# Image chunks in pairs in a fused attention and feed-forward kernel: one bank of turned sums, one key product, one copy

## The chip, the cores and the metric

The kernel runs on one core of a Trainium2 chip. The metric is the device time of one execution in microseconds (us), quoted as the median of several runs. The span that the profile shows is about 1.8 us shorter than the timed figure of the same run.

## The reference

```python
kv_pool = kv.reshape(B, H // 4, 4, W // 4, 4, C).mean(axis=(2, 4))   # B=4, H=384, W=32, C=128
k = v = kv_pool.reshape(B, -1, C) @ w_sr                             # 768 keys per image
a = softmax(q @ k.T / sqrt(C))                                       # q: 12288 tokens per image
x = a @ v
out = (relu(x @ w_gate) * (x @ w_val)) @ w_out                       # 128 -> 1536 -> 128
```

Each image of 384 by 32 pixels is averaged over 4 by 4 squares to 768 keys, in six chunks of 128. Each key serves as its own value. 49152 tokens attend to the keys of their image and go through a gated feed-forward layer.

## The kernel before

Tokens go in 96 tiles of 512. For a tile, TensorE makes six score blocks (one per image chunk), ScalarE takes the exponential, TensorE weights the values, and later turns them through the feed-forward layer (12 value products, 12 gate products, 48 output products). A chunk must be pooled before any score: its pixels lie as 16 blocks of 128x128 (four image lines times four columns) to be added, turned so that channels lie on partitions, multiplied by `w_sr`, scaled into keys, and turned back into values.

```python
def add_lines(eng, b, jc, i):                  # sums of image lines, one chunk
    ...
    eng.tensor_tensor(s2[:, i], parts[:, 2 * i], parts[:, 2 * i + 1], op=ALU.add)
    ...
def turn_pooled(b, jc, pooled):                # TensorE turns and adds what is left, one bank a chunk
    tp = bank([128, 128])
    n = pooled.shape[1]
    for i in range(n):
        nc.tensor.matmul(tp, pooled[:, i, :], ident, is_transpose=True,
                         start=(i == 0), stop=(i == n - 1))
    keep_turned(b, jc, tp)                     # copy on VectorE
def project(b, jc):                            # key product, then keep_keys: scaled copy on VectorE
    key_banks[b, jc] = bank([128, 128])
    nc.tensor.matmul(key_banks[b, jc], w_sr_f32, kv_Ts.pop((b, jc)), start=True, stop=True)
...
def keep_values(k, half, copy=nc.vector.tensor_copy):
    ...
    nc.vector.reciprocal(rinvs[k][:, own], x_ps[:, :, C])
    if half == 1:
        ...
        nc.vector.tensor_tensor(inv2s[k][:, :, 0], rinv, rinv, op=ALU.mult)   # the squaring
```

In the start, where nothing else is ready, TensorE turns and adds all 16 blocks of chunks 0 and 1 of image 0, the lines of chunks 2 to 5 are summed on VectorE first (one sum on GpSimd), and the scores of four tiles are made chunk by chunk. In the steady part the next image is pooled on GpSimd while tiles 16 to 21 of an image's 24 take the pooled chunks in.

The softmax here doesn't subtract the row's maximum and nothing guards it: scores larger than these inputs give would overflow.

## Time and profile before

| | before |
|---|---|
| time, median of 3 (lowest, highest) | 1053.98 us (1052.41, 1054.56) |
| span of the profiled run | 1051.8 us |
| first exponential; first value product of the feed-forward layer | 14.42; 34.84 us |
| a tile without, with image work | 10.51; 10.90 us |
| squarings on VectorE, 128x4 | 96, least 161, median 163, most 1218 ns |

The first value product marks the end of the start: from there TensorE goes tile by tile. A tile's length is read from its first value product to that of the next. The columns of a line in part 5 of the page are the line, engine and operation, the shapes, the count, then busy us and mean ns of one, then the idle time ahead of it.

### The profile page before, as it was taken

The page shows a single profiled execution, that of the slowest core. Times are in us where ns is not written, and L with a number is a line of the kernel's source. Part 1 is how long each engine was busy: PE and PEld are TensorE (multiplying, and loading weights), DVE is VectorE, ACT ScalarE, POOL GpSimd, SP SyncE. Part 2 cuts the span into 40 slices and gives each one's busy share as a digit, 9 for nine tenths or more (in the row PEclk, how much of TensorE's full clock was granted, in tenths as well). Part 3 has the DMA queues.
Part 4 walks back from the last instruction along what each step waited for, and adds up shares of the span by engine and source line. Part 5 has one row for each costly group of instructions (what it writes and reads, how often), then busy time and mean ns, then how long its engine had stood idle before and what let it go on. Part 6 is the DMA issues. An engine that isn't in the chain of part 4 may idle for free.

```text
span 1051.8 us, 26213 instructions
## 1 busy us (share of the span) xinstructions
PE 1035.5 (98%) x9988; PEld 690.8 (66%) x9988; DVE 922.1 (88%) x1803; ACT 911.8 (87%) x1758; POOL 107.2 (10%) x127
## 2 busy tenths in 40 slices
PE   7999999999999999999999999999999999999997
PEld 4666666666666666666666666666666666666664
DVE  3798989898989898998989898999898989898996
ACT  3988888888888888888888888888888888888886
POOL 2000045200000015400000003340000000000000
PEclk9999999999999999999999999999999999999999
DMA  8843356231322335523224134542341423222111
GB/s 293 126 81 67 74 187 161 57 86 32 86 53 66 71 126 143 154 52 72 66 52 86 32 86 130 169 125 50 72 84 33 87 51 67 51 46 51 46 32 46
DMA packets 125710, 90.76 MB, mean 86 GB/s; under 512 B 103312, under 2 KB 103952, under 8 KB 125584
## 3 DMA queue, kind: packets, MB, share of 16 engines
q1 hardware_dynamic: 120144, 75.85, 27.4%
q0 software_dynamic: 5440, 13.24, 7.7%
q8 instruction: 78, 1.28, 0.5%
q14 instruction: 48, 0.39, 0.1%
HBM read 52.76 MB, written 25.17 MB: 74 GB/s over the span
## 4 chain that ended last, share of the span: by engine, by line
PE 96%; DMA 2%; DVE 1%; ACT 1%; issue 0%; SPq 0%; ACTq 0%; DVEq 0%
PE bank_ps L270 24%; PE bank_ps L256 24%; PE bank_ps L245 24%; PE bank_ps L212 12%; PE bank_ps L200 12%; DMA parts<-in_kv_dram 2%; PE bank_ps L155 0%; PE bank_ps L180 0%; ACT aT L201 0%; DVE hT L259 0%; DVE kv_s L141 0%; ACT o_sb L280 0%; DVE kv_s L138 0%; PE bank_ps L189 0%; DVE x L221 0%
## 5 line engine op out<-in xcount | busy, mean ns | idle before, releaser
L259 DVE SCALAR_TENSOR_TENSOR hT<-bank_ps,val 128x512 f16<-128x512 f32 x1152 | 765.4, 687 | 98.9 <-ACT val L249 70.4
L249 ACT CAST val<-bank_ps 128x512 f16<-128x512 f32 x1152 | 678.0, 590 | 118.0 <-PE bank_ps L245 115.7
L270 PEld LDWEIGHTS <-hT 128*128 128x128 f16 x4608 | 351.0, 98 | 206.3 <-DVE hT L259 2.9
L270 PE MATMUL bank_ps<-wo,hT 128*128 128x128 f16 x4608 | 443.6, 219 | 2.1 <-DVE hT L259 2.0
L245 PE MATMUL bank_ps<-xT,wv 128*128 128x512 f16 x1152 | 436.9, 379 | 0.4 <-ACT x L221 0.4
L256 PE MATMUL bank_ps<-xT,wg 128*128 128x512 f16 x1152 | 435.9, 378 | 0.9 <-DVE hT L259 0.8
L201 ACT ACTIVATE aT<-bank_ps 128x512 f16<-128x512 f32 x576 | 346.2, 604 | 5.8 <-PE bank_ps L200 5.3
L212 PE MATMUL bank_ps<-kv,aT 128*128 128x129 f16 x2304 | 223.7, 220 | 0.0
L212 PEld LDWEIGHTS <-aT 128*128 128x128 f16 x2304 | 177.5, 98 | 68.1 <-issue 0.4
L200 PE MATMUL bank_ps<-qT,kv 128*128 128x512 f16 x576 | 217.6, 381 | 2.7 <-DVE qT L110 1.5
L256 PEld LDWEIGHTS <-wg 128*128 128x128 f16 x1152 | 111.5, 97 | 65.4
L245 PEld LDWEIGHTS <-wv 128*128 128x128 f16 x1152 | 112.7, 98 | 0.6 <-issue 0.5
L221 DVE CAST x<-bank_ps 128x256 f16<-128x256 f32 x186 | 77.2, 415 | 2.1 <-PE bank_ps L212 2.1
L77 POOL DMA_DIRECT2D q<-in_q_dram x23 | 12.5, 543 | 551.0 <-DMA qT<-q 550.8
L138 POOL TENSOR_TENSOR kv_s<-parts 128x512 f32<-128x512 f32 x37 | 46.6, 1271 | 166.3 <-DMA parts<-in_kv_dram 163.9
L282 DVE TENSOR_TENSOR o_sb<-bank_ps,inv 128x512 f32<-128x512 f32 x93 | 63.3, 681 | 0.0
L200 PEld LDWEIGHTS <-kv 128*128 128x128 f16 x576 | 56.4, 98 | 5.5 <-DVE qT L110 2.2
L222 DVE RECIPROCAL rinv<-bank_ps 128x2 f32<-128x2 f32 x192 | 30.8, 160 | 1.0 <-ACT x L221 0.7
L141 POOL TENSOR_TENSOR kv_s<-kv_s 128x512 f32<-128x512 f32 x18 | 22.8, 1268 | 1.4
L226 DVE TENSOR_TENSOR inv<-rinv 128x4 f32<-128x4 f32 x96 | 18.5, 192 | 3.3
L176 DVE COPY kvT<-bank_ps 128x128 f32<-128x128 f32 x24 | 6.8, 284 | 9.4 <-PE bank_ps L166 5.1
L146 POOL TENSOR_TENSOR s<-kv_s 128x256 f32<-128x256 f32 x18 | 13.1, 726 | 1.4
(41 smaller groups left out, 102.0 us busy)
## 6 DMA issues: line engine op xcount, KB each, us to landing
parts<-in_kv_dram SPq DMA_DIRECT2D x48, 512.0 KB, 6.4
out_dram<-o_sb SPq DMA_DIRECT2D x96, 256.0 KB, 2.2
q<-in_q_dram POOLq DMA_DIRECT2D x23, 512.0 KB, 5.2
xT<-x SPq DMA_TRANSPOSE x94, 2.4
q<-in_q_dram SPq DMA_DIRECT2D x1, 768.0 KB, 8.5
wv<-in_moe_w_val_dram POOLq DMA_DIRECT2D x2, 192.0 KB, 4.3
wg<-in_moe_w_gate_dram POOLq DMA_DIRECT2D x2, 192.0 KB, 5.0
wo<-in_moe_w_out_dram POOLq DMA_DIRECT2D x1, 384.0 KB, 9.7
```

The source lines that it names most:

```text
L138: eng.tensor_tensor(s2[:, i], parts[:, 2 * i], parts[:, 2 * i + 1], op=ALU.add)
L200: nc.tensor.matmul(s_ps, kv16[:, k // NST, jc, 0:C], qT_of(k), start=True, stop=True)
L201: nc.scalar.activation(aTs[k][:, jc, :], s_ps, AF.Exp, scale=qk_scale)
L212: nc.tensor.matmul(x_ps[:, i, :], aTs[k][:, jc, s * 128 : (s + 1) * 128], kv16[:, k // NST, jc, C : 2 * C + 1], start=(jc == 0 and i == 0) ...
L221: copy(x16s[k][:, own, :], x_ps[:, :, 0:C])
L222: nc.vector.reciprocal(rinvs[k][:, own], x_ps[:, :, C])
L245: nc.tensor.matmul(va_ps, wv16[:, fb * 128 : (fb + 1) * 128], xTs[k], start=True, stop=True)
L249: nc.scalar.copy(val, va_ps)
L256: nc.tensor.matmul(g_ps, wg16[:, fb * 128 : (fb + 1) * 128], xTs[k], start=True, stop=True)
L259: nc.vector.scalar_tensor_tensor(hTs[k][:, fb, :], g_ps, 0.0, vals.pop((k, fb)), op0=ALU.max, op1=ALU.mult)
L270: nc.tensor.matmul(o_ps[:, s, :], hTs[k][:, fb, s * 128 : (s + 1) * 128], wo16[:, fb, :], start=(fb == 0 and s == 0), stop=(fb == NFB - 1) ...
L282: nc.vector.tensor_tensor(o_sb, o_ps, inv2.to_broadcast([128, NS, 128]), op=ALU.mult)
```

## The change

Its intent: fewer handovers in the start. Two chunks share a bank of turned sums, a key product of 256 columns and each copy. In pair 0 TensorE turns and adds all lines; in pairs 1 and 2 other engines add lines 0 and 1 and TensorE turns lines 2 and 3 as they land. The casts of the first queries and, in the start, the copies of values go from ScalarE to VectorE. The scores of the last pair are made tile by tile, so that tile 0 is finished while the others' exponentials run. In the steady part the same functions run per pair, in 9 tiles instead of 18.

```diff
-        nc.scalar.copy(q16, q32s[i])
+        nc.vector.tensor_copy(q16, q32s[i])
...
+    def turn_open(b, pair):
+        kv_Ts[b, pair] = bank([128, 2, 128])
+    def turn_add(b, pair, lines, first=False, final=False):
...        # for both chunks h and all columns i
+                nc.tensor.matmul(kv_Ts[b, pair][:, h], lines[:, h, i], ident, is_transpose=True, ...)
+        if final:
+            nc.vector.tensor_copy(kvT, kv_Ts[b, pair])
+    def project(b, pair):
+        pr = bank([128, 2, 128])
+        nc.tensor.matmul(pr, w_sr_f32, kv_Ts.pop((b, pair)), start=True, stop=True)
+        nc.vector.tensor_scalar(kv16[:, b, 2 * pair : 2 * pair + 2, 0:C], pr, 1.0 / (r * r), None, ...)
...        # the start, pair 1 (pair 2 alike, with GpSimd and VectorE)
+    s2 = add_lines(1, (nc.vector, nc.vector))
+    turn_open(0, 1)
+    turn_add(0, 1, s2, first=True)
+    attend(0, 0)
+    turn_add(0, 1, line(1, 2))
+    turn_add(0, 1, line(1, 3), final=True)
+    attend(1, 0)
+    project(0, 1)
...        # the last pair, tile by tile
+    for jc in range(4, NJC):
+        scores(0, jc)
+    turn_values(0, 2)
+    for jc in range(4, NJC):
+        scores(1, jc)
+    attend(0, 2)
...
```

More of the change, by code (lines that the diff above doesn't have):

```diff
@@ L127, in kv_load @@
             nc.sync.dma_start(parts[:, dh].rearrange("p h dw c -> p (h dw c)"), rows[dh])
-        for h in range(2):
-            kv_in[b, 2 * pair + h] = parts[:, :, h]
-    s2s, s1s, kv_Ts, key_banks = {}, {}, {}, {}
-    def add_lines(eng, b, jc, i):
-        if i == 0:
-            s2s[b, jc] = work.tile([128, 2, r, C], FP32, tag="kv_s2", bufs=2, name="kv_s2")
-        parts, s2 = kv_in[b, jc], s2s[b, jc]
-        if i < 2:
-            eng.tensor_tensor(s2[:, i], parts[:, 2 * i], parts[:, 2 * i + 1], op=ALU.add)
-        else:
-            s1s[b, jc] = work.tile([128, r, C], FP32, tag="kv_s1", bufs=2, name="kv_s1")
-            eng.tensor_tensor(s1s[b, jc], s2[:, 0], s2[:, 1], op=ALU.add)
-            del kv_in[b, jc], s2s[b, jc]
@@ L144, in pool_columns @@
-    def pool_columns(eng, s1):
-        s2 = work.tile([128, 2, C], FP32, tag="kv_c2")
-        eng.tensor_tensor(s2, s1[:, 0:2], s1[:, 2:4], op=ALU.add)
-        s3 = work.tile([128, 1, C], FP32, tag="kv_c1", bufs=3)
-        eng.tensor_tensor(s3, s2[:, 0:1], s2[:, 1:2], op=ALU.add)
-        return s3
-    def turn_pooled(b, jc, pooled):
-        tp = bank([128, 128])
-        n = pooled.shape[1]
-        for i in range(n):
-            nc.tensor.matmul(
-                tp, pooled[:, i, :], ident, is_transpose=True,
-                start=(i == 0), stop=(i == n - 1),
-            )
-        keep_turned(b, jc, tp)
@@ L161, in turn_lines @@
-    def turn_lines(b, pair):
-        tps = [bank([128, 128]) for _ in range(2)]
-        for dh in range(r):
-            for h in range(2):
-                for dw in range(r):
-                    nc.tensor.matmul(
-                        tps[h], kv_in[b, 2 * pair + h][:, dh, dw, :], ident, is_transpose=True,
-                        start=(dh == dw == 0), stop=(dh == dw == r - 1),
-                    )
-        for h in range(2):
-            del kv_in[b, 2 * pair + h]
-            keep_turned(b, 2 * pair + h, tps[h])
@@ L174, in keep_turned @@
-    def keep_turned(b, jc, tp):
-        kv_Ts[b, jc] = work.tile([128, 128], FP32, tag="kvT", bufs=3, name="kvT")
-        nc.vector.tensor_copy(kv_Ts[b, jc], tp)
-    def project(b, jc):
-        key_banks[b, jc] = bank([128, 128])
-        nc.tensor.matmul(key_banks[b, jc], w_sr_f32, kv_Ts.pop((b, jc)), start=True, stop=True)
-    def keep_keys(b, jc):
-        nc.vector.tensor_scalar(
-            kv16[:, b, jc, 0:C], key_banks.pop((b, jc)), 1.0 / (r * r), None, op0=ALU.mult
-        )
-    def turn_values(b, jc, copy):
-        vt = bank([128, 128], FP16)
-        nc.tensor.transpose(vt, kv16[:, b, jc, 0:C], ident16)
-        copy(kv16[:, b, jc, C : 2 * C], vt)
@@ L193, with pool_pixels @@
-    aTs, x_banks, x16s, xTs, rinvs, inv2s = {}, {}, {}, {}, {}, {}
+        kv_in[b, pair] = parts
+    s3s, kv_Ts, key_banks = {}, {}, {}
+    def pool_pixels(eng, b, pair, h):
+        parts = kv_in[b, pair]
+        s2 = work.tile([128, 2, r, C], FP32, tag="kv_s2", bufs=2)
+        for i in range(2):
+            eng.tensor_tensor(s2[:, i], parts[:, 2 * i, h], parts[:, 2 * i + 1, h], op=ALU.add)
+        s1 = work.tile([128, r, C], FP32, tag="kv_s1", bufs=2)
+        eng.tensor_tensor(s1, s2[:, 0], s2[:, 1], op=ALU.add)
+        c2 = work.tile([128, 2, C], FP32, tag="kv_c2", bufs=2)
+        eng.tensor_tensor(c2, s1[:, 0:2], s1[:, 2:4], op=ALU.add)
+        if h == 0:
+            s3s[b, pair] = work.tile([128, 2, C], FP32, tag="kv_s3", bufs=2, name="kv_s3")
+        eng.tensor_tensor(s3s[b, pair][:, h], c2[:, 0], c2[:, 1], op=ALU.add)
@@ new lines, in turn_open @@
+    def turn_open(b, pair):
+        kv_Ts[b, pair] = bank([128, 2, 128])
+    def turn_add(b, pair, lines, first=False, final=False):
+        n = lines.shape[2]
+        for h in range(2):
+            for i in range(n):
+                nc.tensor.matmul(
+                    kv_Ts[b, pair][:, h], lines[:, h, i], ident, is_transpose=True,
+                    start=(first and h == i == 0), stop=(final and i == n - 1),
+                    skip_group_check=True,
+                )
+        if final:
+            kvT = work.tile([128, 2, 128], FP32, tag="kvT", bufs=2)
+            nc.vector.tensor_copy(kvT, kv_Ts[b, pair])
+            kv_Ts[b, pair] = kvT
@@ new lines, in project, with turn_values @@
+    def project(b, pair):
+        pr = bank([128, 2, 128])
+        nc.tensor.matmul(pr, w_sr_f32, kv_Ts.pop((b, pair)), start=True, stop=True)
+        nc.vector.tensor_scalar(
+            kv16[:, b, 2 * pair : 2 * pair + 2, 0:C], pr, 1.0 / (r * r), None, op0=ALU.mult
+        )
+    def turn_values(b, pair):
+        vt = bank([128, 2, 128], FP16)
+        for h in range(2):
+            nc.tensor.transpose(vt[:, h], kv16[:, b, 2 * pair + h, 0:C], ident16)
+        nc.vector.tensor_copy(kv16[:, b, 2 * pair : 2 * pair + 2, C : 2 * C], vt)
@@ L194 @@
+    aTs, x_banks, x16s, xTs, rinvs, inv2s, sums = {}, {}, {}, {}, {}, {}, {}
     hTs, o_banks, vals = {}, {}, {}
@@ L216, in values, with keep_values @@
             )
-    def keep_values(k, half, copy=nc.vector.tensor_copy):
+    def keep_values(k, half, copy=nc.vector.tensor_copy, now=True):
         own = slice(2 * half, 2 * half + 2)
@@ L221, in keep_values, with keep_sums @@
         copy(x16s[k][:, own, :], x_ps[:, :, 0:C])
-        nc.vector.reciprocal(rinvs[k][:, own], x_ps[:, :, C])
-        if half == 1:
-            rinv = rinvs.pop(k)
-            inv2s[k] = work.tile([128, NS, 1], FP32, tag="inv2", bufs=8, name="inv2")
-            nc.vector.tensor_tensor(inv2s[k][:, :, 0], rinv, rinv, op=ALU.mult)
+        sums[k, half] = x_ps[:, :, C]
+        if now:
+            keep_sums(k, half)
+    def keep_sums(k, half):
+        nc.vector.reciprocal(rinvs[k][:, 2 * half : 2 * half + 2], sums.pop((k, half)))
+        if half == 0:
+            return
+        rinv = rinvs.pop(k)
+        inv2s[k] = work.tile([128, NS, 1], FP32, tag="inv2", bufs=8, name="inv2")
+        nc.vector.tensor_tensor(inv2s[k][:, :, 0], rinv, rinv, op=ALU.mult)
     def x_turn(k):
@@ L318, with attend, line, add_lines @@
         nc.tensor.matmul(idle, ident16, ident16, start=True, stop=True)
-    def attend(jc, tiles=(0, 1)):
-        for k in tiles:
+    def attend(k, pair):
+        for jc in (2 * pair, 2 * pair + 1):
             for half in range(2):
                 values(k, jc, half)
+    def line(pair, dh):
+        return kv_in[0, pair][:, dh]
+    def add_lines(pair, engines):
+        s2 = work.tile([128, 2, r, C], FP32, tag="kv_s2", bufs=2)
+        for h in range(2):
+            engines[h].tensor_tensor(
+                s2[:, h], line(pair, 0)[:, h], line(pair, 1)[:, h], op=ALU.add
+            )
+        return s2
     q_cast(0)
     q_turn_pe(0)
+    turn_open(0, 0)
+    for dh in range(r):
+        turn_add(0, 0, line(0, dh), first=dh == 0, final=dh == r - 1)
+    project(0, 0)
     for i in range(1, GRP):
         q_cast(i)
-    turn_lines(0, 0)
-    for jc in range(2):
-        project(0, jc)
-        keep_keys(0, jc)
-    add_lines(nc.vector, 0, 2, 0)
     for jc in range(2):
         scores(0, jc)
-        turn_values(0, jc, nc.scalar.copy)
+    turn_values(0, 0)
     for i in range(1, GRP):
         q_turn_pe(i)
-    for jc in range(2):
-        for k in range(1, GRP):
+    for k in range(1, GRP):
+        for jc in range(2):
             scores(k, jc)
-    attend(0)
-    add_lines(nc.vector, 0, 3, 0)
-    add_lines(nc.vector, 0, 2, 1)
-    add_lines(nc.vector, 0, 2, 2)
-    turn_pooled(0, 2, s1s.pop((0, 2)))
-    attend(1, [0])
-    add_lines(nc.vector, 0, 3, 1)
-    project(0, 2)
-    add_lines(nc.vector, 0, 3, 2)
-    keep_keys(0, 2)
-    add_lines(nc.gpsimd, 0, 4, 0)
+    s2 = add_lines(1, (nc.vector, nc.vector))
[6 more added lines that the diff above has]
+    project(0, 1)
+    for k in range(GRP - 1):
+        for jc in range(2, 4):
+            scores(k, jc)
+        if k == 0:
+            turn_values(0, 1)
+    s2 = add_lines(2, (nc.gpsimd, nc.vector))
     for own in (slice(0, D_FF // 2), slice(D_FF // 2, D_FF)):
@@ L359 @@
     q_load(2)
-    for jc in range(2, NJC):
-        scores(0, jc)
-        turn_values(0, jc, nc.scalar.copy)
-        ahead = jc + 1 < NJC
-        if ahead:
-            turn_pooled(0, jc + 1, s1s.pop((0, jc + 1)))
-        for k in range(1, GRP):
-            scores(k, jc)
-        if ahead:
-            project(0, jc + 1)
-        if jc == 2:
-            add_lines(nc.vector, 0, 5, 0)
-            add_lines(nc.vector, 0, 4, 1)
-        if jc == 3:
-            add_lines(nc.vector, 0, 5, 1)
-        if ahead:
-            keep_keys(0, jc + 1)
-        if jc in (2, 3):
-            add_lines(nc.vector, 0, jc + 2, 2)
-        attend(jc - 1, (0, 1) if jc > 2 else [1])
+    turn_open(0, 2)
+    turn_add(0, 2, s2, first=True)
+    turn_add(0, 2, line(2, 2))
+    turn_add(0, 2, line(2, 3), final=True)
+    for jc in range(2, 4):
+        scores(GRP - 1, jc)
+    attend(0, 1)
+    project(0, 2)
+    attend(1, 1)
+    for jc in range(4, NJC):
+        scores(0, jc)
+    turn_values(0, 2)
+    for jc in range(4, NJC):
+        scores(1, jc)
+    attend(0, 2)
     for half in range(2):
-        values(0, NJC - 1, half)
-        keep_values(0, half)
-    for jc in range(NJC - 1):
-        values(2, jc, 0)
+        keep_values(0, half, now=False)
+    for jc in range(4, NJC):
+        scores(2, jc)
     x_turn_pe(0)
     for half in range(2):
-        values(1, NJC - 1, half)
-        keep_values(1, half, nc.scalar.copy)
-    left = [(2, NJC - 1, 0)]
+        keep_sums(0, half)
+    for jc in range(4, NJC):
+        scores(3, jc)
+    attend(1, 2)
+    for half in range(2):
+        keep_values(1, half)
+    for jc in range(NJC - 2):
+        values(2, jc, 0)
+    left = [(2, jc, 0) for jc in range(NJC - 2, NJC)]
     left += [(k, jc, half) for k, half in ((3, 0), (2, 1), (3, 1)) for jc in range(NJC)]
     last = NT + LAG - 1
-    kv_s3 = {}
     for k in range(LAG, last + 1):
@@ L434 @@
                 if step == 3 and 0 <= at - 2 < NJC:
-                    for i in range(3):
-                        add_lines(nc.gpsimd, b, at - 2, i)
-                    kv_s3[b, at - 2] = pool_columns(nc.gpsimd, s1s.pop((b, at - 2)))
-                if 0 <= at - 4 < NJC:
+                    pool_pixels(nc.gpsimd, b, (at - 2) // 2, at % 2)
+                pair = (at - 5) // 2
+                if at % 2 == 1 and 0 <= pair < NJC // 2:
                     if step == 5:
-                        turn_pooled(b, at - 4, kv_s3.pop((b, at - 4)))
+                        turn_open(b, pair)
+                        turn_add(b, pair, s3s.pop((b, pair))[:, :, None], True, True)
                     if step == 7:
-                        project(b, at - 4)
-                        keep_keys(b, at - 4)
+                        project(b, pair)
                     if step == 9:
-                        turn_values(b, at - 4, nc.vector.tensor_copy)
+                        turn_values(b, pair)
             if k == last and step >= 2:
```

## The prediction

> **What bounds the kernel now.** I read the page first (busy shares, chain of waits), then busy time by windows, then the timeline of the first 45 us with the waits of that stretch. The page's engine line and chain:
>
> ```profile
> PE 1035.5 (98%) x9988; PEld 690.8 (66%) x9988; DVE 922.1 (88%) x1803; ACT 911.8 (87%) x1758; POOL 107.2 (10%) x127
> ...
> PE 96%; DMA 2%; DVE 1%; ACT 1%; issue 0%; SPq 0%; ACTq 0%; DVEq 0%
> ```
>
> TensorE is busy for 1035.5 of 1051.8 us and holds 96% of the chain. Because matmul ends are modelled I do not take busy for full use; the windows say more. Columns: stretch, its length, busy us and instructions of each engine, granted clock, DMA share, GB/s.
>
> ```profile
> 104.35:114.86 10.51, 10.51 (x105) 6.97 (x103) 9.40 (x19) 9.37 (x19) 0.00 (x0) 1.00 0.30 66
> 178.58:189.48 10.90, 10.90 (x109) 7.47 (x107) 9.91 (x22) 9.38 (x19) 8.15 (x8) 1.00 0.40 88
> 0.00:34.84 34.84, 26.06 (x203) 18.22 (x203) 13.37 (x35) 17.58 (x38) 6.70 (x16) 0.95 0.91 265
> ```
>
> The first two are one token tile each in the steady part, from first value product to first value product: 10.51 us without image work, 10.90 us with one image chunk, TensorE full in both. The third is the start, up to the first value product at 34.84 us: there TensorE is idle for 8.8 us. So two places can be touched by this change: 18 chunks of 0.39 us in the steady part, where only TensorE's own time counts, and the start, where waits count. Nothing else in the 1012 us after 34.84 is in the diff.
>
> The start from the timeline (start us, duration, engine, line, what, idle before and its releaser):
>
> ```profile
> 17.02 0.68 DVE L138 TENSOR_TENSOR kv_s<-parts 128x512 f32<-128x512 f32 x1
> ...
> 22.17 0.61 PE L200 MATMUL bank_ps<-qT,kv 128*128 128x512 f16 x1 [0.97 <-DVE kv L183]
> ...
> 22.81 0.60 ACT L201 ACTIVATE aT<-bank_ps 128x512 f16<-128x512 f32 x1 [2.86 <-PE bank_ps L200]
> ...
> 34.38 0.65 ACT L221 CAST x<-bank_ps 128x256 f16<-128x256 f32 x2 [0.70 <-PE bank_ps L212]
> ...
> 35.25 0.58 ACT L249 CAST val<-bank_ps 128x512 f16<-128x512 f32 x1 [0.22 <-PE bank_ps L245]
> ```
>
> ScalarE has 24 exponentials to do before the first value copy at 35.25. It waits 2.86 us for chunk 2, 0.63 us within it, and 0.48, 0.39 and 0.35 us more from there to chunk 5, since each chunk needs its own turn, copy, product and copy. The last exponential starts at 33.0. Only then do tile 0's last copies and its turn reach the first value product. The image lines are not what holds this: by the trace's completion marks pair 1's land at 14.13, 15.40, 16.69, 17.98 and pair 2's at 20.36, 21.63, 22.88, 24.12.
>
> [...]
>
> ```profile
> 18.63:22.04 3.41, 1.34 (x11) 0.99 (x10) 2.53 (x6) 1.33 (x3) 0.24 (x1) 1.00 0.92 364
> 22.04:25.46 3.42, 3.29 (x14) 2.23 (x15) 1.56 (x4) 2.01 (x5) 3.42 (x6) 0.50 0.35 52
> 8.40:11.80 3.40, 2.86 (x23) 2.38 (x23) 0.12 (x1) 0.00 (x0) 0.00 (x0) 1.00 1.02 414
> ```
>
> A window with 1.34 us of work is followed by 3.4 us at 0.50, in which scores start 0.43 us apart instead of 0.216. [...]the third line, filled by 32-bit transposes alone, stays at 1.00 and so does what follows[...]. [...]a pair's copy costs about 0.42 us against 2 x 0.29. [...]
>
> **The change part by part. Steady part.** Turn, product and turn of one chunk are 0.109 + 2 x 0.112 + 0.056 = 0.389 us by the starts of successive matmuls, exactly the 0.39 above: it is pure streaming. A pair streams the same columns: 2 x 0.109 + 2 x 0.215 + 2 x 0.056 = 0.76 against 0.78. Nine pairs give 0.2 us. VectorE saves (6 x 0.28 - 0.42 - 0.42 - 0.28) = 0.6 us a pair, on an engine with an eighth of its time free: worth 0.
>
> **Start.** I walk the changed order by hand with before's durations: 32-bit transposes 0.109 us apart with 0.27 to the result, scores 0.216 apart and 0.39 to the result, four value products 0.23, exponentials 0.48 apart when queued and 0.60 alone, handovers 0.04 (to VectorE or ScalarE) and 0.06 (to TensorE). Removed on ScalarE: three casts (it ran them until 14.5, which held the first exponential back to 14.42) and six value copies at 0.25. Removed on VectorE: 7 + 4 line sums, replaced by three of 0.69. Added on TensorE: the 16 transposes of chunks 2 to 5 become 2 x 24, i.e. 32 x 0.109 = 3.5 us more.
>
> Pair 0: last line 10.94, turned 12.08, copied 12.53, product (2 x 0.215 plus latency) 13.28, keys 13.73, first exponential 14.22 (before 14.42). [...]the other six exponentials run from 15.85 (before 16.91) to 18.85.
>
> Pair 1: VectorE's two sums end at 16.64 and 17.24; TensorE turns them by 17.73, attends tile 0 (0.45), turns lines 2 and 3 by 20.1; copy 20.56, product 21.3, keys 21.76, exponential 22.25. Before, chunk 2 alone came at 22.81 and chunk 3 at 26.25. The window before 22.04 now holds about 2.4 us of TensorE work instead of 1.34, so I expect no half clock. Six exponentials start at 22.25, 22.73, 23.2, 23.7, 24.2, 24.65.
>
> Pair 2: four PSUM banks hold the open sums of tiles 0 and 1, four are left. In the built program the bank of pair 2's sum is that of the third of these scores (tile 1, chunk 2), free at 23.8. From there 24 transposes take 2.62 us: 26.63, although the last line landed at 24.12. Copy 27.09; meanwhile tile 3's two pair-1 scores and attention; product 28.06, keys 28.5, score 28.96, exponential 29.0. Eight exponentials in a row now: the last starts at 29.0 + 7 x 0.48 = 32.4 and ends at 32.98. Tile 0 finishes beneath them: attended 30.6, copied 31.2, turned 31.6, copied back 32.07. TensorE ends the third and fourth tile's scores at 31.8, tile 1's values at 32.26, four chunks of tile 2's at 32.7, and starts the first value product there. Against 34.84 that is 2.14 us. One more value pair in the first loop costs 0.1.
>
> Sum: 2.14 - 0.1 + 0.2 = 2.2 us. The rest of the program is bound by TensorE at the same rate and its inputs (weights landed by 30.8 and 35.5) come early enough, so the lead survives to the end. 1053.98 - 2.2 = 1051.8.
>
> **Rivals.** First, the extra transposes become the bound: if the clock is halved while they run, or if the s2 sums arrive late, each batch of 24 costs up to 2.6 us more, and the start is no shorter. For it: they sit on the path from 23.8 to 26.6. Against: TensorE is well filled in each 3.4 us window of the walk. Result about 1054. Second, the bank does not bind and the last line does: turned at 25.2, first exponential at 27.4, value product near 31.0, a gain of 3.9 us and 1050.1. For it: it is the floor that the landings set; against: the bank sequence of the build. [...]Fourth, steady stalls vanish with fewer handovers: tiles 15, 61 and 65 took 0.2 to 0.7 us extra, 1.3 in all; they look random, and I give this nothing.
>
> **Range and chances.** The walk gives 1051.8; floor and clock rivals give 1050.1 and 1054. Before's own three runs spread by 2.15 us (1052.41 to 1054.56). I take 1050.0 to 1053.4 for 8 in 10. A 2% gain would need 21 us, and only 8.8 us of TensorE's idle time lies in the start, so faster by 2% is 0.01; slower by 2% would need a steady loss of 0.2 us on every tile, 0.01.
>
> **What would show it.** Right: first value product near 32.7; eight exponentials 0.48 apart just ahead of it; no dip of the granted clock between 5 us and the end; [...]pair 2's first transpose right after an exponential ended, not after a DMA; image tiles in the steady part still 0.38 to 0.39 above 10.51. Wrong: transposes 0.21 apart; a steady tile with image work at 10.6 or at 11; pair 2's turn starting with its line at 24.1; TensorE idle over 1 us between 25 and 32.

The forecast's sum was 2.14 - 0.1 + 0.2 = 2.2 us, from 1053.98 to 1051.8. How long a 128x512 cast takes on VectorE was the author's estimate (no trace before the change has one; ScalarE's took 0.617 us). A pair's copy of 0.42 us can be had from the trace before: VectorE's 128x256 casts out of PSUM (L221) took 415 to 424 ns, its copies of 128x128 to keys and turned sums 0.29 us each in the start.

## More of the kernel before

The line `inv2 = rinv * rinv` squares the inverse softmax sum; that square scales the output, since the layer is homogeneous of degree two.

```profile
L226 DVE TENSOR_TENSOR inv<-rinv 128x4 f32<-128x4 f32 x96 | 18.5, 192 | 3.3
```

A mean of 192 beside a median of 163 (least 161, most 1218 ns) says that a few of the 96 took far longer, and that this is counted as busy time, not as a wait.

## The result, and the profile after

The changed kernel took 1051.84 us (median of 4 runs, 1050.71 to 1053.17) and the kernel before, beside it, 1053.46 (4 runs, 1052.41 to 1054.56). The ratio is 0.9985, with a 95% interval of 0.9968 to 1.0002. A ratio is the mean time of one kernel's runs over that of the other's in the same rounds, so it is not quite the ratio of the medians. Predicted were 1051.8, and 0.98 that the change stays within 2%. The total came out, though the gain itself is 1.6 us where 2.2 had been forecast, with an interval that reaches zero. What follows asks whether it came out for the reasons given.

The page's engine line and its chain of waits:

```profile
PE 1038.3 (99%) x9996; PEld 692.5 (66%) x9996; DVE 919.5 (87%) x1771; ACT 908.6 (86%) x1746; POOL 107.3 (10%) x127
...
PE 97%; DVE 1%; ACT 1%; DMA 0%; issue 0%; SPq 0%; ACTq 0%; DVEq 0%
```

TensorE is busy for 2.8 us more in a span 0.5 us shorter, and the 2% of the chain that transfers had are gone. The busy time by windows of the changed kernel (the start, the two windows around which the clock fell before, a plain tile, a tile with a pair's work, and tile 17):

```profile
0.00:33.06 33.06, 28.41 (x226) 22.04 (x227) 9.89 (x29) 13.48 (x26) 6.72 (x16) 1.00 0.97 279
18.63:22.04 3.41, 2.74 (x25) 2.18 (x23) 0.85 (x2) 0.35 (x1) 1.88 (x2) 1.00 0.92 362
22.04:25.46 3.42, 3.06 (x20) 1.91 (x21) 0.89 (x2) 2.99 (x6) 3.42 (x7) 1.00 0.86 131
134.23:144.75 10.52, 10.52 (x106) 6.97 (x103) 9.41 (x19) 9.39 (x19) 8.94 (x9) 1.00 0.43 99
210.46:221.74 11.28, 11.28 (x111) 7.38 (x109) 10.17 (x20) 9.96 (x20) 0.00 (x0) 1.00 0.13 38
176.84:188.66 11.82, 11.43 (x111) 7.71 (x109) 11.02 (x22) 9.49 (x19) 8.69 (x10) 1.00 0.48 80
```

The start ends at 33.06 instead of 34.84. The window from 18.63 holds 2.74 us of TensorE work instead of 1.34, and the next one keeps its full clock. A pair costs 11.28 - 10.515 = 0.765 us against 2 x 0.385 before. The last line is the odd one: tile 17 has the same 111 matmuls as the tile above it, and takes 0.54 us longer, with TensorE not full.

ScalarE's part of the start, from the timeline (start, duration, engine, line, operation, count, idle before and its releaser):

```profile
14.42 1.08 ACT L185 ACTIVATE aT<-bank_ps 128x512 f16<-128x512 f32 x2 [12.19 <-PE bank_ps L184]
15.94 3.04 ACT L185 ACTIVATE aT<-bank_ps 128x512 f16<-128x512 f32 x6 [0.43 <-PE bank_ps L184]
22.47 3.04 ACT L185 ACTIVATE aT<-bank_ps 128x512 f16<-128x512 f32 x6 [3.49 <-PE bank_ps L184]
...
29.32 4.03 ACT L185 ACTIVATE aT<-bank_ps 128x512 f16<-128x512 f32 x8 [0.98 <-PE bank_ps L184]
33.48 0.59 ACT L239 CAST val<-bank_ps 128x512 f16<-128x512 f32 x1
```

The eight last exponentials run in one row, as predicted. From the first exponential to the first value product it is 33.06 - 14.42 = 18.64 us, and 34.84 - 14.42 = 20.42 before. I call this the stretch. It is the better measure of the start, for the first exponential itself came anywhere from 13.40 to 14.83 in the ten profiles of the changed kernel and its variants. Part of that spread has a cause. TensorE's transposes of pair 0 on the changed kernel:

```profile
6.63 5.63 PE L153 MATMUL bank_ps<-ident,parts 128*128 128x128 f32 x32 [0.19 <-DMA parts<-in_kv_dram]
```

They start 0.213 us apart, twice the 0.109 of the kernel before, until the trace's first record of the full clock at 10.60 us; in the kernel before it stands at 4.98. (The windows view prints 1.00 ahead of the first record too.) So the last line of pair 0, landed at 10.44, was copied only at 12.29. In a variant below (the half-sum run), where the same line landed at 10.45 and the full clock came at 5.33, the copy began at 11.63 and the first exponential at 13.75 instead of 14.42.

But 1.78 us won by the first value product should still be there later. It is not: the first value product of the last tile starts at 1034.12 us before and at 1034.07 after. Adding up the tiles' excess over 10.515 us gives 8.35 us before, of which 18 x 0.385 are image work and 1.42 are not; after, it gives 10.01, of which 9 x 0.765 are image work and 3.13 are not. Those 3.13 us sit in six tiles (15, 17, 37, 39, 61, 63). What is slow in them is the squaring. Here is its line on the page after, then both timelines around tile 15, first the changed kernel's:

```profile
L216 DVE TENSOR_TENSOR inv<-rinv 128x4 f32<-128x4 f32 x96 | 20.8, 217 | 3.3
```

```profile
156.05 1.27 POOL L136 TENSOR_TENSOR s<-parts 128x512 f32<-128x512 f32 x1 [1.84 <-DMA parts<-in_kv_dram]
...
156.28 1.06 DVE L216 TENSOR_TENSOR inv<-rinv 128x4 f32<-128x4 f32 x1
...
157.26 1.28 DVE L249 SCALAR_TENSOR_TENSOR hT<-bank_ps,val 128x512 f16<-128x512 f32 x2
157.40 1.27 POOL L138 TENSOR_TENSOR s<-s 128x512 f32<-128x512 f32 x1
...
157.99 0.38 PE L246 MATMUL bank_ps<-xT,wg 128*128 128x512 f16 x1 [0.38 <-DVE hT L249]
```

And the kernel before:

```profile
157.41 1.27 POOL L138 TENSOR_TENSOR kv_s<-parts 128x512 f32<-128x512 f32 x1 [1.95 <-DMA parts<-in_kv_dram]
...
157.94 0.76 DVE L226 TENSOR_TENSOR inv<-rinv 128x4 f32<-128x4 f32 x1
```

The squaring of 4 columns, 161 ns when alone, starts inside a GpSimd sum of 128x512 and ends about 20 ns after it. Both read two inputs from SBUF. VectorE's gate product (L249, one input in PSUM) lies beside GpSimd's next sum and keeps its 0.69 us (two overlapping ones make 1.28). TensorE then waits 0.38 us for the gate products, which come late behind the squaring. The arithmetic closes in every tile: the squaring comes 1.01 us into a tile; where GpSimd's sum began 0.48 us into it, 0.48 + 1.27 - 1.01 = 0.74 us are left, and the squaring took 0.76 (tile 15 before); begun at 0.79, it gives 1.05 against 1.06 (tile 15 after). Where the sum began at 1.03 or later, the squaring had started first and took 0.16.

The two profiles agree throughout: all ten squarings that started inside a GpSimd sum (four before, six after) took 602 to 1218 ns and ended 17 to 23 ns after it, and no other took over 165. Of the gate products 212 started inside such a sum, and none took over 693 ns; the longest of all of them is 693 too. The traces show this delay, not what makes it.

### The profile page after: what moved, and what is told of

Its sections match the earlier page's. It is cut to its first block, busy times and chain, and to the rows that moved or that the text cites. A ratio compares the mean times of both kernels' runs of the same rounds, so it can differ in the third digit from the quotient of the medians. Undisturbed runs are those within 1.5% of the kernel's fastest.

```text
span 1051.3 us, 26110 instructions
## 1 busy us (share of the span) xinstructions
PE 1038.3 (99%) x9996; PEld 692.5 (66%) x9996; DVE 919.5 (87%) x1771; ACT 908.6 (86%) x1746; POOL 107.3 (10%) x127
## 3 DMA queue, kind: packets, MB, share of 16 engines
q8 instruction: 78, 1.28, 0.5%
## 4 chain that ended last, share of the span: by engine, by line
PE 97%; DVE 1%; ACT 1%; DMA 0%; issue 0%; SPq 0%; ACTq 0%; DVEq 0%
PE bank_ps L260 24%; PE bank_ps L246 24%; PE bank_ps L235 23%; PE bank_ps L196 12%; PE bank_ps L184 12%; PE bank_ps L153 1%; PE bank_ps L165 1%; DVE hT L249 1%; DMA parts<-in_kv_dram 0%; ACT aT L185 0%; DVE o_sb L272 0%; ACT val L239 0%; ACT o_sb L270 0%; DVE kv L166 0%; DVE x L205 0%
## 5 line engine op out<-in xcount | busy, mean ns | idle before, releaser
L249 DVE SCALAR_TENSOR_TENSOR hT<-bank_ps,val 128x512 f16<-128x512 f32 x1152 | 764.7, 687 | 100.1 <-ACT val L239 71.6
L136 POOL TENSOR_TENSOR s<-parts 128x512 f32<-128x512 f32 x36 | 45.3, 1269 | 166.4 <-DMA parts<-in_kv_dram 132.4
L216 DVE TENSOR_TENSOR inv<-rinv 128x4 f32<-128x4 f32 x96 | 20.8, 217 | 3.3
L138 POOL TENSOR_TENSOR s<-s 128x512 f32<-128x512 f32 x18 | 22.8, 1268 | 1.4
L160 DVE COPY kvT<-bank_ps 128x256 f32<-128x256 f32 x12 | 5.0, 418 | 11.7 <-PE bank_ps L153 11.7
L140 POOL TENSOR_TENSOR c<-s 128x256 f32<-128x256 f32 x18 | 13.1, 727 | 1.4
```

Of the source, the lines that this page charges most:

```text
L136: eng.tensor_tensor(s2[:, i], parts[:, 2 * i, h], parts[:, 2 * i + 1, h], op=ALU.add)
L249: nc.vector.scalar_tensor_tensor(hTs[k][:, fb, :], g_ps, 0.0, vals.pop((k, fb)), op0=ALU.max, op1=ALU.mult)
```

## The experiments

My first theory: the start gained what was predicted, and the steady part took it back, because the squaring meets GpSimd's sums more often. A rival: the extra stalls are ordinary unevenness of this program, or TensorE's own. A third question is what the start's gain consists of.

**The changed kernel again, as it was.**

> The changed kernel once more, for the spread. [...]the profile shows again about six squarings (of 128x4) of 0.8 to 1.2 us instead of 0.16, all in tiles 15, 17, 37, 39, 61, 63, and the same 3 us lost in the steady part. If those stalls are random, they sit in other tiles and their sum is anything from 0 to 4 us. First value product 32.5 to 33.1 us either way. Time about 1051.5.

It took 1052.38 us, ratio 0.9984 (0.9972 to 0.9997). Four squarings were slow (tiles 15, 17, 61, 65) and the excess that isn't image work was about 1.75 us. The stretch was 18.64 again. The expectation was half met: three of its six tiles, and 1.75 us instead of 3. (The first value product, at 33.47, was later than expected; the full clock first came at 11.04 here.) So the loss is there in each profile but varies, as GpSimd's sums start when their image lines land (in the changed kernel from 44 us on, 17 of its waits for them, 132.4 us in all, were ended by the lines' transfer).

**The squaring on ScalarE, in the changed kernel and in the kernel before.** There the instruction reads the inverse sum once, and it comes a tile later, at step 5, well before its use.

```diff
-        nc.vector.tensor_tensor(inv2s[k][:, :, 0], rinv, rinv, op=ALU.mult)
+        if k < GRP:
+            nc.vector.tensor_tensor(inv2s[k][:, :, 0], rinv, rinv, op=ALU.mult)
+        else:
+            to_square.append((k, rinv))
...
+            if step == 5 and to_square:
+                kV, rinv = to_square.pop()
+                nc.scalar.activation(inv2s[kV][:, :, 0], rinv, AF.Square)
```

> The changed kernel with the squaring moved from VectorE to ScalarE, so that VectorE has no instruction with two inputs in SBUF in the steady part. [...]no steady tile is over 11.30 us, tiles without image work all 10.51 to 10.52, about 3.1 us less than the profile of the changed kernel, so about 1049 timed (2 us under the changed kernel of the same rounds). Rival (stalls of another cause, e.g. transfers or instruction fetch): stalls stay, time within 0.5 us of the changed kernel.

> The same edit in the kernel before. [...]its 1.4 us of steady stalls go, about 1052 timed against 1053.5. The difference to the changed kernel with the same edit is then the gain of the start alone: 1.7 to 2.2 us by the prediction's walk. Rival (the change saves or costs in the steady part too): a difference outside 1.2 to 2.7 us.

Changed kernel: 1050.05 us, ratio 0.9962 (0.9949 to 0.9976). Kernel before: 1052.24, ratio 0.9981 (0.9969 to 0.9994). In both profiles every tile without image work is 10.51 to 10.52 us long. Tile 17 of the changed kernel, the one that had taken 11.82:

```profile
176.31:187.59 11.28, 11.28 (x111) 7.71 (x109) 10.13 (x21) 9.48 (x20) 8.68 (x10) 1.00 0.44 84
```

It is full, at 11.28. This settles the cause of the stalls: the squaring's place on VectorE cost 1052.38 - 1050.05 = 2.33 us in the changed kernel and 1054.09 - 1052.24 = 1.85 us in the kernel before (medians of the same rounds; the second figure also holds chance in how often the clock fell, see below). With it out of the way the change is worth 1052.24 - 1050.05 = 2.19 us, as much as the prediction had said, where it is 1.71 us with it in. Whether the change really meets more sums, or whether six against four was chance, is not settled: the difference of the two costs, 0.5 us, is inside the intervals, and two more profiles of the changed kernel have four and five slow squarings. All other runs below carry this edit, so that tiles do not blur them.

**The image loads three steps later, to shift the sums away from the squaring.**

```diff
-                if step == 1 and 0 <= at < NJC and at % 2 == 0:
+                if step == 4 and 0 <= at < NJC and at % 2 == 0:
```

> The changed kernel with the steady part's image loads issued 3 steps (2.6 us) later in their tile, squaring left on VectorE. [...]the second sum of each pair now starts near 3.4 us in its tile instead of 0.8, so the squaring at 1.01 us into tiles 15, 17 and so on is free; instead the sums run over into the next tile and can hold its squaring for 0.4 us at most. Stalls sum to under 2 us instead of 3.1; about 1050.5. Rival (stalls come from the loads themselves): they stay 0.5 us each and just move.

A miss, and the fault is the experiment's. It took 1051.53 us (0.9976), and the stalls stayed in tiles 15, 17, 37, 61 and 63: in the program no other transfer is issued on that queue between the two steps (in the changed kernel's trace the loads go out at 147.05 us, behind a transfer issued at 145.78, and the next is issued at 155.86). So the queue's order is the same. It is worth one more repeat of the changed kernel (stretch 18.64, again), and nothing on the question.

**The last pair chunk by chunk instead of tile by tile.**

```diff
-    for jc in range(4, NJC):
-        scores(0, jc)
-    turn_values(0, 2)
-    for jc in range(4, NJC):
-        scores(1, jc)
+    for k in range(GRP):
+        scores(k, 4)
+        if k == 0:
+            turn_values(0, 2)
+    for k in range(2):
+        scores(k, 5)
...
```

> Undoes one part: the last pair's scores again chunk by chunk over all four tiles, not tile by tile. Base is the changed kernel with the squaring on ScalarE (first value product at 33.08 us, 1048.2 us in its profile). My theory: tile 0's second exponential of the pair is now the sixth in the queue region instead of the second, its copies, turn and copy back then come after the exponentials: first value product about 1.2 us later, 34.2 to 34.4. Rival (the order is worth nothing because the first value copy waits for the last exponential anyway): 33.1.

1051.13 us, ratio 0.9971 (0.9959 to 0.9983). ScalarE's timeline in this run:

```profile
29.65 3.04 ACT L186 ACTIVATE aT<-bank_ps 128x512 f16<-128x512 f32 x6 [0.98 <-PE bank_ps L185]
32.91 0.60 ACT L186 ACTIVATE aT<-bank_ps 128x512 f16<-128x512 f32 x1 [0.22 <-PE bank_ps L185]
33.93 0.60 ACT L186 ACTIVATE aT<-bank_ps 128x512 f16<-128x512 f32 x1 [0.42 <-PE bank_ps L185]
35.05 0.59 ACT L243 CAST val<-bank_ps 128x512 f16<-128x512 f32 x1 [0.53 <-PE bank_ps L239]
```

Tile 0 gets its fifth and sixth chunk later, so the first value product comes at 34.64 and ScalarE runs dry three times around it (0.22, 0.42 and 0.53 us). The stretch is 19.90 us, 1.26 longer. So the order tile by tile is worth 1.26 us.

**The casts of the first queries back on ScalarE.**

```diff
-        nc.vector.tensor_copy(q16, q32s[i])
+        nc.scalar.copy(q16, q32s[i])
```

> Undoes the move of the four casts to VectorE alone, on the same base. By the walk that I predicted with, the casts on ScalarE hold the first exponential back by 0.2 us. Against it, four profiles of the changed kernel have the first exponential at 13.95 to 14.83, before at 14.25 and 14.42, so I now expect nothing: first exponential in that same band, stretch 18.5 to 18.8, time that of the base. If the casts matter the stretch is 0.2 us or more off.

```profile
12.88 1.66 ACT L100 CAST q16s<-q 128x512 f16<-128x512 f32 x3 [7.30 <-DMA q<-in_q_dram]
14.44 1.07 ACT L186 ACTIVATE aT<-bank_ps 128x512 f16<-128x512 f32 x2
```

1049.81 us, ratio 0.9967 (0.9954 to 0.9981), the same as with the casts on VectorE. The exponential starts right behind the casts, so they do hold it, by about 0.2 us. But VectorE, free of them, begins the copies of the queries 1.46 us after the first copy of keys instead of 1.55, and the sums 2.46 instead of 2.54, and the stretch is 18.40. That is 0.24 us under the base, just over the mark that was set for "the casts matter", but it counts the held-back exponential as a gain. Counted from the start of the first scaled copy of keys (13.36 us here) to the first value product it is 32.84 - 13.36 = 19.48 us, against 33.06 - 13.51 = 19.55 in the changed kernel. The move was worth nothing.

**More of the lines summed on VectorE.** First lines 2 and 3 added there, so that TensorE turns 16 blocks of a pair and not 24; then all four, which leaves 8.

```diff
+    s3 = add_last(1)                      # VectorE: line 2 + line 3, both chunks of pair 1
...
-    turn_add(0, 1, line(1, 2))
-    turn_add(0, 1, line(1, 3), final=True)
+    turn_add(0, 1, s3, final=True)        # pair 2 alike; all four lines: s3 holds s2 too
```

> Undoes half of one part, on the same base: VectorE sums lines 2 and 3 of pairs 1 and 2 (two more sums of 0.69 us a pair) and TensorE turns 16 blocks a pair instead of 24. My theory, that the extra transposes lie on the path while VectorE idles: pair 1's keys about 0.65 us earlier, pair 2's about 0.8, first value product near 32.3 and about 0.8 us less in all. Rival (VectorE's sums take the place on the path): 33.1 or later.

> Undoes the whole of that part, on the same base: VectorE sums all four lines, TensorE turns 8 blocks a pair. Four sums of 0.6 to 0.69 us now follow the last line: pair 1's keys about 0.4 us later than with 24 blocks, pair 2's about the same, first value product 32.9 to 33.6. So TensorE's summing is worth up to 0.5 us against none, and less than half of it is better than both. Rival (transposes are what costs): faster than the half version, under 32.

Half: 1049.17 us, ratio 0.9953 (0.9941 to 0.9965), stretch 18.11.

```profile
13.75 1.08 ACT L186 ACTIVATE aT<-bank_ps 128x512 f16<-128x512 f32 x2 [11.52 <-PE bank_ps L185]
...
28.12 4.03 ACT L186 ACTIVATE aT<-bank_ps 128x512 f16<-128x512 f32 x8 [2.21 <-PE bank_ps L185]
```

The last row of eight starts 14.37 us after the first exponential, against 14.90 in the changed kernel. So 0.53 us were gained where 0.8 had been expected, all of it in pair 2: pair 1's exponentials start 8.04 us after the first, as before (8.05). (In pair 2 this edit also puts tile 3's two scores ahead of the last turn.) All: 1052.49 us, ratio 0.9983, stretch 21.12, where at most 0.4 more had been expected. The windows of that run tell it:

```profile
17.25:20.66 3.41, 0.76 (x7) 0.42 (x4) 2.44 (x5) 1.68 (x4) 0.00 (x0) 1.00 1.02 406
20.66:24.08 3.42, 2.94 (x14) 2.16 (x14) 0.81 (x3) 0.00 (x0) 1.78 (x2) 0.50 0.34 135
```

While VectorE adds, TensorE has 0.76 us of work in 3.41, and the next window, with the turns and the key product of pair 1, runs at half clock. The exponentials of pair 1 start 10.50 us after the first, not 8.05: the whole loss is there. About 1.0 us of it is the half clock: the last four transposes take 1.12 us instead of 0.63, and from the copy of the turned sums to that of the keys it is 1.82 instead of 1.28. The other 1.4 us are ahead of it: the last line landed 0.65 us later, and VectorE's sums end only at 20.93, 2.84 us after that landing.

**Filling TensorE in the kernel before, to take the clock's part by itself.** Products of two identities that nothing reads, in the gaps of the start of the kernel before (with its squaring on ScalarE): 32 of them first, then 38 at other places (the diff shows these).

```diff
+    idle2 = bank([128, 128])
+    for _ in range(18):                   # ahead of the other tiles' first scores
+        nc.tensor.matmul(idle2, ident16, ident16, start=True, stop=True)
...                                        # and 10 each behind attend(0) and project(0, 2)
```

> The kernel before (squaring on ScalarE) with 32 small filler products where TensorE waits between 18.5 and 22 us, to keep the clock up; image work unchanged. If the dip of the granted clock to 0.50 for 3.4 us costs before about 1 us on the path: no dip in the profile and first value product about 0.9 us earlier than 35.30, near 34.4. Rival (dip costs nothing on the path): 35.2. What is left against 33.08 is then the worth of pairs and order.

> The filler experiment again, with fewer fillers, each in a stretch where TensorE waits longer than they take (18 near 15 us, 10 near 18.7, 10 near 21.2), since in the first attempt the dip came earlier, the fillers themselves ran at half clock and a VectorE sum met a GpSimd sum for 0.6 us. Dip theory: no dip between 5 and 35 us, and the stretch from first exponential to first value product is about 0.9 us under the 20.42 and 21.05 of the two profiles with a dip, 19.5 to 20.0. Rival (the dip is off the path): 20.4 or more without a dip. If the dip stays, the question stays open.

The first attempt failed: it gave 1052.94 us (0.9986), and the fall of the clock only moved, to a window in which some of the fillers ran at half speed.

```profile
17.14:20.55 3.41, 3.41 (x22) 2.34 (x23) 1.84 (x3) 2.71 (x6) 0.00 (x0) 0.50 1.03 410
```

The second held the clock, as its windows show:

```profile
18.40:21.80 3.40, 2.58 (x32) 2.09 (x30) 2.52 (x6) 1.29 (x3) 0.21 (x1) 1.00 0.99 394
21.80:25.20 3.40, 2.36 (x17) 1.52 (x17) 2.09 (x6) 2.29 (x5) 3.40 (x6) 1.00 0.32 50
```

Its stretch is 33.97 - 14.13 = 19.84 us, against 20.42 and 21.05 in the two profiles of the unfilled kernel that had the fall. But the second of these, with the squaring on ScalarE, has something else in its start:

```profile
20.91 1.26 POOL L138 TENSOR_TENSOR kv_s<-parts 128x512 f32<-128x512 f32 x1 [19.13 <-DMA parts<-in_kv_dram]
...
21.03 1.68 DVE L141 TENSOR_TENSOR kv_s<-kv_s 128x512 f32<-128x512 f32 x1
```

VectorE's sum, with two inputs in SBUF, begins 0.12 us after GpSimd's and takes 1.68 us instead of 0.69, ending 0.54 us after GpSimd's: a delay like the squaring's. It is chunk 3's sum, and the copy of chunk 2's keys queues behind it. The first failed attempt had one too (1.30 us). So 20.42 is the fair base, and against 18.64 the start's gain of 1.78 us splits into 0.6 us because the clock no longer falls and 1.2 us from the order and the pairs. The order alone was worth 1.26 us above, so the pairs gave the start little but the kept clock. This rests on one profile each.

The timed ratio, 0.9981, is that of the unfilled kernel, but the two stand over different runs of the kernel before, and these are not alike. Each timed run lists its mean granted clock:

| mean clock of a run | runs of the kernel before, of 38 in four rounds | mean time |
|---|---|---|
| 0.999 or 1.000 | 7 | 1052.7 us |
| 0.997 or 0.998 | 14 | 1053.6 us |
| 0.995 or 0.996 | 17 | 1055.1 us |

One fall takes 0.0016 off the mean (3.41 us at 0.50, of 1051.8), and the half clock at the program's end takes 0.0011 before and 0.0014 after in the first two profiles, so 0.996 or less points to more than one fall. All nine runs of the changed kernel say 0.999 (mean 1052.2 us), and so do all five of the filled one, against one in five of the unfilled. So the kernel before lost its clock in most of its runs, and beside the seven in which it did not, the changed kernel leads by only about 0.5 us while its squaring stays on VectorE. This sorts runs after the fact and is no experiment, but it says that much of the timed gain is the kept clock.

**The key product chunk by chunk again, the rest in pairs.**

```diff
-        pr = bank([128, 2, 128])
-        nc.tensor.matmul(pr, w_sr_f32, kv_Ts.pop((b, pair)), start=True, stop=True)
-        nc.vector.tensor_scalar(kv16[:, b, 2 * pair : 2 * pair + 2, 0:C], pr, ...)
+        prs = [bank([128, 128]) for _ in range(2)]
+        for h in range(2):
+            nc.tensor.matmul(prs[h], w_sr_f32, kvT[:, h], start=True, stop=True)
+        for h in range(2):
+            nc.vector.tensor_scalar(kv16[:, b, 2 * pair + h, 0:C], prs[h], ...)
```

> Undoes the pairing of the key product alone, on the changed kernel with the squaring on ScalarE: two products of 128 columns into two banks and two copies to keys a pair; the turned sums stay one bank and one copy. From the first exponential to the first value product the three base profiles all need 18.64 us. My theory, that pairing this step is no gain on the path (the second chunk's product and the longer copy delay the first chunk's keys): the first exponential of pairs 1 and 2 comes about 0.35 us earlier after its sums are turned, and the stretch is 18.2 to 18.5; the steady part is unchanged. Rival (pairing is what shortens the start): 19 us or more.

1049.15 us, ratio 0.9960 (0.9947 to 0.9972), stretch 18.30, 0.34 shorter. VectorE's copies of pair 1 (turned sums, then keys):

```profile
19.88 0.42 DVE L160 COPY kvT<-bank_ps 128x256 f32<-128x256 f32 x1 [2.96 <-PE bank_ps L153]
20.95 0.52 DVE L169 TENSOR_SCALAR kv<-bank_ps 128x128 f16<-128x128 f32 x2 [0.64 <-PE bank_ps L167]
```

The first copy of keys starts 1.07 us after the copy of the sums, and the exponential at 21.72, so 1.84 us from copy to exponential. With one product per pair (from the run with half the lines) these were 19.60, 20.88 and 21.79: 1.28 and 2.19. One of the change's pairings costs time on the chain: the first score needs one chunk, and the pair makes it wait for two. In the timed ratios the step (0.9962 to 0.9960) is too small to see.

**Both improvements together.** The edits of the half-sum run and of this one.

> Three edits together on the changed kernel: the squaring on ScalarE, lines 2 and 3 of pairs 1 and 2 summed on VectorE (16 blocks turned instead of 24), and the key product chunk by chunk in two banks with two copies. Measured one at a time on the squared kernel they shortened the stretch from the first exponential to the first value product (18.64 us) by 0.53 (the sums) and 0.34 (the products). Theory: the two shorten different links of the same chain (the turn ahead of the copy, the copy and product behind it), so they add: stretch 17.8 us, median about 1048.7, ratio to before 0.995. Rival: they overlap, since the stretch is also held by TensorE, which is nearly full there, or by ScalarE's 24 exponentials: stretch 18.1 as with the sums alone, median 1049.2. No slow squaring and no dip of the granted clock in either.

```profile
13.40 1.09 ACT L189 ACTIVATE aT<-bank_ps 128x512 f16<-128x512 f32 x2 [11.17 <-PE bank_ps L188]
...
27.53 4.03 ACT L189 ACTIVATE aT<-bank_ps 128x512 f16<-128x512 f32 x8 [1.97 <-PE bank_ps L188]
```

1048.75 us (1048.35 to 1049.6, 5 runs), ratio 0.9944 (0.993 to 0.9957). The first value product comes at 31.27, a stretch of 17.87: the two gains add (18.64 - 0.53 - 0.34 = 17.77 was expected). This beats both kernels. Its lead over the half-sum run alone (0.9953) is within the intervals, and the kernel before was slow in this round (mean 1054.9 us, against 1053.4 to 1054.2 in the other three).

## Why the prediction was right or wrong

The figure was right, 1051.84 against 1051.8, but two of its zeros were not. The parts, from the first pair of profiles and from the pair with the squaring on ScalarE (gain in us):

| part | predicted | first pair | squaring on ScalarE |
|---|---|---|---|
| start, to the first value product | 2.14 | 34.84 - 33.06 = 1.78 | 35.30 - 33.08 = 2.22 |
| first loop, one more value pair | -0.1 | -0.11 | -0.11 |
| image work in the steady part | 0.2 | 0.05 | 0.05 |
| squarings behind GpSimd's sums | 0 | 1.42 - 3.13 = -1.71 | 0 |
| end of the program | 0 | 0.44 | 0.44 |
| sum | 2.2 | 0.45 | 2.60 |
| spans | | 0.49 | 2.63 |

- Start. The mechanism was right: no fall of the clock, eight exponentials 0.48 apart just ahead of the value product, an extra of 32 transposes that fits. The end of it was 0.36 us late (33.06 against 32.7). 0.20 of that came in at once, with the first exponential at 14.42 and not 14.22. The walk took pair 0's transposes at 0.109 us from before's trace, and "no dip" from 5 us on; they ran 0.213 apart until 10.60, which was one of the listed signs of being wrong. It cost about 0.67 us (14.42 against 13.75 in the half-sum run), of which an earlier landing of the last line, 10.44 instead of 10.94, gave back most. The 2.22 of the last column is not cleaner than the 1.78: it holds the 0.6 us that a blocked sum cost the kernel before there.
- Casts. They took 0.42 us each on VectorE (420 to 428 ns). Their removal from ScalarE was counted as bringing the first exponential forward, and it does, by about 0.2 us; but what VectorE does next is about 0.1 us later, and to the first value product nothing is gained (19.55 against 19.48 us).
- Bank. I said the third exponential of pair 1 would hold pair 2's turn by its bank. It is named as releaser, but TensorE was idle only 0.205 us there (predicted start 23.8, measured 24.19). TensorE's own queue held it at least as much (the weight load there came after 0.73 us for which the trace names no releaser), and fewer blocks to turn helped by 0.53 us. The second rival's floor was not reached either: the last line had landed at 23.47, and TensorE was busy for 6.75 of the 7.00 us from 25 to 32.
- The first rival's ground (transposes as the bound) proved half true: TensorE summing all last lines is not the best split. But the other end of the scale, all of it on VectorE, is 2.5 us worse: about 1.0 at half clock, behind the window with 0.76 us of TensorE work, the rest because of VectorE's sums in a row.
- Pairing. I treated one product per pair as free in the start. By its stretch it costs 0.34 us there. In the steady part I had 0.2 us of gain from it; it is 0.05. Fewer, longer instructions took TensorE as long: 0.765 us a pair against 2 x 0.385.
- The fourth rival is the step that failed. It named tiles 15, 61 and 65 and put their stalls down as "random", worth nothing. They were 1.42 us in four tiles (37 was the fourth), they had one cause, and after the change they were 3.13 us in six. That they lay where GpSimd was pooling an image, and that the squaring's mean stood above its median, was there to be seen.
- End of the program. The last GpSimd drain of the closing sequence starts 0.35 us after the clearing of the semaphores before, and 0.03 us after it in the changed kernel; it also takes 0.17 us instead of 0.04. With the squaring on ScalarE it is the same: from the start of ScalarE's last row of outputs to the end of the span it is 4.54 us before and 4.13 after (4.57 and 4.12 in the first pair). It was not predicted, and its cause was not sought.

So the total was right partly by luck: in the first pair of profiles the squarings ate the start's whole gain, and the end of the program gave most of the rest. In the timed runs the mix varies (the ratios 0.9985, 0.9984 and 0.9976 are gains of 1.6, 1.7 and 2.5 us), and without the squarings the change is worth 2.19 us. That this is the forecast sum is luck as well: the profiles of that pair hold 0.44 us from the end of the program and 0.6 from the blocked sum, which the forecast did not have.

## What to carry to other kernels

A short instruction whose mean lies above its median is worth a look at its longest cases and at what ran beside them on the other engines; here a delayed instruction counted as busy (1218 ns instead of 161), and the view of waits named only what came behind it. Before one profile is taken as the base of a split, look through its stretch for such cases, and through the clocks of the timed runs. A gain in one stage must be looked for again at the end of the next one. Pair what only streams, but not the link on which the first result waits, and look at TensorE's clock when work is moved off it: here a window of 3.41 us with 0.76 of its work was followed by one at 0.50.

## What the traces show of the clock and the end, and what stays open

- In the changed kernel the 3.41 us ahead of 10.60 us hold nothing but 32-bit transposes, 0.213 us apart; from there they run 0.109 apart and the record of the granted clock says 1.00.
- Each fall lasted 3.41 us. Windows of that length with 0.76 us of TensorE work (busy as the profile models it; all four lines on VectorE), 1.34 (the kernel before) and 1.70 (the first filler run) were followed by half clock. In steps of 3.413 us from the first full clock, the least filled window ahead of the program's last one that no half clock followed held 1.98 us in the kernel before and 2.38 in the changed one. What lies between is left open.
- The end of the kernel before took 0.44 us longer than that of the changed one with the same work ahead of it, through the last GpSimd drain; the cause stays open.
